# A fused attention and FFN kernel: the second batch's transposes begun one unit later, its loads put ahead of the output weights, and the first FFN unit spread one product per step

## The chip, the cores and the metric

The kernel runs on one core of a Trainium2 chip. The core has separate engines that run their own instruction streams in order: TensorE (PE in the profile; its weight loads PEld), VectorE (DVE), ScalarE (ACT), GpSimd (POOL), and SyncE (SP), which issues transfers. The metric is the device time of one launch in microseconds (us). The kernel before was timed three times: 394.67, 395.43 and 396.14, median 395.43 us.

## The reference

Block-sparse attention over 4 batches of 8 heads, 768 tokens and head size 64, then an RMS norm and a gated FFN over the 3072 tokens (model width 512, hidden width 1536). Cut to what is computed:

```python
scores = scale * np.matmul(q, k.transpose(0, 1, 3, 2))
# mask: neighbouring, first, last and sampled blocks of 32
scores = np.where(mask, scores, -1000000000.0)
scores = scores - np.max(scores, axis=-1, keepdims=True)
attn = np.exp(scores)
attn = attn / (np.sum(attn, axis=-1, keepdims=True) + 1e-09)
attn_out = np.matmul(attn, v)
...
x = attn_out.transpose(0, 2, 1, 3).reshape(B * S, H * D)
rms = np.sqrt(np.mean(x * x, axis=-1, keepdims=True) + 1e-06)
xn = x / rms * rms_g
g = xn @ w_gate
silu = g * (1.0 / (1.0 + np.exp(-g)))
val = xn @ w_val
out = silu * val @ w_out
```

Inputs and output are float32; the kernel's loads turn them into bf16 on the way in.

## The kernel before

**Units and steps.** A unit is one half (384 query tokens) of one batch: 8 units, u = 2b + half. In a unit there are four head pairs, so n = 4u + pair runs from 0 to 31. For each n there are six key tiles of 128, and each (n, tile) is a *step*: 192 steps, step = 6n + tile. `qk_exp` does a step's attention: two matmuls (the *score pair*, L243) into a tile `s_`, and one exponential on ScalarE (L247) into `pt`. Tiles `s_` come from the pool `ps_s`, which has two buffers (the *score buffers*), taken in turn; a third request waits until the first holder has been read.

**What a step carries beside its score pair.** A table `fixed`, filled by `at(step, cost, function, ...)`, lists the work that belongs to certain steps:

- `transposes(b, pr)` turns a head pair's q and k into the layout that the score pairs read: 24 small PE matmuls (L165) into a score buffer (tile `tqk`) and two copies on VectorE into `X` (L174). With `early` (batch 0) it uses the FFN's two buffers instead (tiles `tq`, `tk`, copies L171). `X` has six slots; pair pr of batch b is read from step 6(8b + pr) on.
- `av` and `zsum`, one step after a pair's last tile: the product with v (L264), copied to `osb` (L269) and squared by GpSimd (L270), and the sums of the exponentials (L280).
- `norm_a` to `norm_e`, the unit's normaliser: small matmuls (zt L300, ft L333, fb L351), a chain of small VectorE instructions and one on GpSimd (L315) that ends in FHL (L325), a copy `fs` on ScalarE (L337), and the scaled input `xn` of the FFN (L356). For unit 0 these use the FFN's buffers, for later units the score buffers. For unit u they stand at steps 24u + 28 to 24u + 36.
- `load_qk` and `load_v`, the transfers of a later batch, issued by GpSimd (L72, L73, L77).

**The FFN.** A *product* is a call of `ff_g` (four matmuls into `gp`, a tanh on ScalarE L375, `uu` on VectorE L377), `ff_v` (four into `vp`, `hp` on VectorE L391) or `ff_y` (three of the twelve matmuls of an output tile into `yp`, then `yo` and its store). `gp` and `vp` have one buffer each. Unit u's products go into a queue at step 37 + 24u (START is 37), 24 of `ff_g` and `ff_v`, and from u = 1 on the 12 `ff_y` of the unit before. In each step the scheduler takes products off the queue by a *credit*: every step adds a rate worked out from the estimated costs, and all work subtracts its cost (0.34 for a score pair, 0.65 for a product). `RESERVE` keeps five products in the queue while there are attention steps. In units after the first, a step is also filled until its estimated work reaches 0.9.

**The order of the engines.** All instructions are written out in this order, and each engine runs its own in that order. Thus a PE instruction that waits for a transfer holds up every score pair behind it.

**The loads.** All loads of inputs but two small ones are issued by GpSimd into one queue (`software_dynamic`): batch 0's q, k and v, then the gate and value weights wg and wv in two halves each (`load_w`, L134 and L135), the output weights wo (`load_wo`, L138), and from step 3 on batch 1's q and k. Its v is loaded at step 24. Batch 1's transposes stand at steps 27, 33, 39 and 45; its first score pair is step 48.

Of the kernel before, what the change touches and what calls it, by code (L numbers as in the profile page):

```python
# [17 lines left out]
def kernel(  # L18
# [114 lines left out]
    def load_w(i):  # L133
        nc.gpsimd.dma_start(out=wg[:, :, i * FH:(i + 1) * FH], in_=wgv[:, :, i * FH:(i + 1) * FH])  # L134
        nc.gpsimd.dma_start(out=wv[:, :, i * FH:(i + 1) * FH], in_=wvv[:, :, i * FH:(i + 1) * FH])  # L135

    def load_wo():
        nc.gpsimd.dma_start(out=wo, in_=moe_w_out.rearrange("(c p) f -> p c f", p=P))  # L138
# [89 lines left out]
    nc.gpsimd.memset(nhalf, -0.5)  # L228
    load_w(0)
    load_w(1)  # L230
    load_wo()

    ptiles, osb, zwt, xns, hps, o2s = {}, {}, {}, {}, {}, {}

    def qk_exp(n, jt):
        u, pr = divmod(n, NP)
        b, ic = divmod(u, 2)
        sl = (b * NP + pr) % NSLOT
        if jt == 0:
            ptiles[n] = ppool.tile([P, NC, 2, TG], BF16, name="pt", tag="pt")  # L240
        s_ = ps_s.tile([P, 2, 512], FP32, name="s_", tag="s")
        for e in range(2):
            nc.tensor.matmul(  # L243
                out=s_[:, e, 0:TG],
                lhsT=X[0:D + NB, sl, e, 1, jt * P:(jt + 1) * P],
                rhs=X[0:D + NB, sl, e, 0, ic * TG:(ic + 1) * TG], start=True, stop=True)
        nc.scalar.activation(  # L247
            out=ptiles[n][:, jt, :, :], in_=s_[:, :, 0:TG], func=AF.Exp, scale=SCALE)
# [167 lines left out]
    NSTEP = NU * NP * NC  # L416
# [4 lines left out]
    def at(step, cost, fn, *a):  # L421
        fixed.setdefault(step, []).append((cost, fn, a))

    for n in range(NU * NP):
        u, pr = divmod(n, NP)
# [12 lines left out]
    at(0, 0, mask_rows, 2, 4)  # L438
    at(4, 0, mask_rows, 4, 2 * NSLOT)
    for b in range(1, B):  # L440
        for pr, sl in enumerate((4, 5, 6, 7) if b == 1 else (2, 4, 6, 7)):
            at(6 * (8 * (b - 1) + sl) + 3, 0.95, transposes, b, pr)
        at(6 * 8 * (b - 1) + 3, 0, load_qk, b, 0, H)
        at(6 * (8 * (b - 1) + 4), 0, load_v, b)

    ffq = []
    for u in range(NU + 1):
# [20 lines left out]
    step, credit = 0, 0.0  # L468
    queue = []
    while True:  # L470
        if step < NSTEP:
            qk_exp(step // NC, step % NC)
            credit -= 0.34
        since = 0.0
        for cost, fn, a in fixed.pop(step, ()):
            fn(*a)
            since += cost
        credit -= since
        u, r = divmod(step - START, 24)
        if u >= 0:  # L480
            if r == 0 and u < len(ffq):
                queue += ffq[u]
                if u == 0:
                    credit = 0.0
            credit += rate.get(u, 99.0)
            keep = RESERVE if step < NSTEP else 0
            while len(queue) > keep and (credit > 0 or (since < 0.9 and step < NSTEP and u > 0)):
                cost, fn, a = queue.pop(0)
                fn(*a)
                credit -= cost  # L490
                since += cost
            if len(queue) <= keep:
                credit = min(credit, 0.0)
        step += 1
        if step >= NSTEP and not fixed and not queue and u >= NU:
            break
# [30 lines left out]
```

## Time and profile before

| | us |
|---|---|
| median of three runs | 395.43 |
| the profiled execution | 396.17 |
| its span, first to last instruction | 394.4 |
| PE busy | 355.1 |
| DVE busy | 211.4 |
| ACT busy | 201.7 |
| POOL busy | 61.2 |

The profile comes from one execution of its own, with the device time and the span given here. Busy times count instructions; a PE matmul's end is modelled, so short gaps between matmuls can be missing or show as busy. In the rows of the timeline, the first number is the start in us from the span's start, the second the length, and the bracket gives how long the engine was idle before and what released it; "x12" is a group of twelve. In the rows of waits stand the waiting and the awaited instruction, the total, the times and the longest. The page's slices are 9.86 us each, in tenths of busy time; PEclk is the granted clock of PE in tenths.

### The profile page before, as it was taken

The numbers are of one execution on the slowest core, as the hardware profiler recorded it, in microseconds if no ns is written. First come the engines' busy times: TensorE is split into PE (matmuls) and PEld (weight loads), VectorE is DVE, ScalarE is ACT, GpSimd is POOL, SyncE is SP. The second block draws the span as 40 slices with busy tenths as digits, with TensorE's granted clock in tenths as the row PEclk, the third lists the DMA queues.
The fourth block names the chain that finished last, engine by engine and source line by source line (L and its number), as shares of the span: only waits on it lengthen the run. The fifth ranks groups of instructions, "written<-read, shape, count | busy, mean of one in ns | idle before, by whom it ended". The sixth has DMA issues, their size and how long they took to land.

```text
span 394.4 us, 6579 instructions
## 1 busy us (share of the span) xinstructions
PE 355.1 (90%) x2700; PEld 189.8 (48%) x2730; DVE 211.4 (54%) x411; ACT 201.7 (51%) x302; POOL 61.2 (16%) x88
## 2 busy tenths in 40 slices
PE   2887068889799999999999999999999999999995
PEld 1443033445355555555555555555555555455552
DVE  5651035655354665556564666556544564587660
ACT  2677035556555555555656565555556656322211
POOL 8952001002101010021001110001000100000000
PEclk9999559999899999999999999999999999999999
DMA  5999950004605100009006000000000000000002
GB/s 72 175 210 208 205 90 2 1 2 68 94 2 71 37 27 2 28 28 161 27 28 107 1 28 13 15 29 27 2 27 29 2 27 28 27 28 27 28 27 106
DMA packets 20257, 20.86 MB, mean 53 GB/s; under 512 B 1284, under 2 KB 17156, under 8 KB 20228
## 3 DMA queue, kind: packets, MB, share of 16 engines
q0 software_dynamic: 16208, 14.16, 23.3%
q1 hardware_dynamic: 4020, 6.30, 4.2%
q8 instruction: 21, 0.34, 0.3%
q14 instruction: 8, 0.07, 0.1%
HBM read 28.31 MB, written 6.29 MB: 88 GB/s over the span
## 4 chain that ended last, share of the span: by engine, by line
PE 72%; DMA 8%; DVE 6%; POOL 5%; ACT 5%; issue 2%; POOLq 0%; DVEq 0%; ACTq 0%
PE gp L371 14%; PE vp L388 14%; PE yp L402 13%; DMA kb<-in_k_dram 7%; PE zw L280 4%; ACT pt L247 3%; DVE xn L356 2%; PE tqk L165 2%; PE oa L264 1%; PE zt L300 1%; PE fb L351 1%; DVE uu L377 1%; ACT th L375 1%; DMA out_dram<-yo 1%; PE vw L388 1%
## 5 line engine op out<-in xcount | busy, mean ns | idle before, releaser
L377 DVE SCALAR_TENSOR_TENSOR uu<-th,gp 128x384 bf16<-128x384 bf16 x90 | 49.8, 554 | 71.0 <-ACT th L375 70.2
L371 PE MATMUL gp<-xn,wg 128*128 128x384 bf16 x360 | 73.2, 326 | 1.4 <-DVE uu L377 1.2
L388 PE MATMUL vp<-xn,wv 128*128 128x384 bf16 x360 | 73.2, 325 | 0.9 <-DVE hp L391 0.9
L402 PE MATMUL yp<-wo,hp 128*128 128x512 bf16 x258 | 70.7, 379 | 1.8 <-issue 0.3
L375 ACT ACTIVATE th<-gp 128x384 bf16<-128x384 f32 x90 | 44.0, 489 | 50.5 <-PE gp L371 49.8
L243 PEld LDWEIGHTS <-X 88*128 88x128 bf16 x384 | 35.3, 100 | 51.1 <-issue 23.9
L391 DVE TENSOR_TENSOR hp<-uu,vp 128x384 bf16<-128x384 bf16 x90 | 49.9, 554 | 17.5 <-PE vp L388 8.7
L371 PEld LDWEIGHTS <-wg 128*128 128x128 bf16 x384 | 36.7, 98 | 32.1 <-issue 3.8
L388 PEld LDWEIGHTS <-wv 128*128 128x128 bf16 x384 | 37.0, 97 | 26.5 <-issue 1.9
L402 PEld LDWEIGHTS <-hp 128*128 128x128 bf16 x288 | 27.6, 97 | 24.9 <-issue 0.8
L174 DVE COPY X<-tqk 64x1536 bf16<-64x1536 bf16 x26 | 24.8, 954 | 24.7 <-PE tqk L165 24.4
L264 PEld LDWEIGHTS <-vb 128*64 128x64 bf16 x384 | 21.5, 114 | 18.1 <-issue 11.1
L280 PE MATMUL zw<-pt,Ez 128*32 128x384 bf16 x384 | 22.4, 341 | 0.0
L165 PE MATMUL tqk<-ident,qb 128*64 128x128 bf16 x156 | 7.5, 236 | 15.0 <-DMA qb<-in_q_dram 14.0
L356 DVE SCALAR_TENSOR_TENSOR xn<-osb,gcol,fb 128x384 bf16<-128x384 f32 x28 | 15.9, 610 | 5.9 <-PE fb L351 5.9
L315 POOL TENSOR_TENSOR rs<-ms,nhalf 128x3 f32<-128x3 f32 x8 | 6.9, 866 | 67.3 <-DVE ms L312 67.3
L411 DVE TENSOR_SCALAR yo<-yp 128x512 f32<-128x512 f32 x21 | 14.4, 686 | 5.4 <-PE yp L402 5.3
L165 PEld LDWEIGHTS <-qb 128*64 128x64 bf16 x192 | 6.8, 119 | 20.1 <-DMA qb<-in_q_dram 14.4
L280 PEld LDWEIGHTS <-Ez 128*32 128x32 bf16 x384 | 7.4, 97 | 12.6 <-issue 11.0
L264 PE MATMUL oa<-pt,vb 128*64 128x384 bf16 x96 | 11.3, 379 | 0.0
L165 PE MATMUL tqk<-ident,kb 128*64 128x128 bf16 x156 | 7.3, 234 | 4.0 <-DMA kb<-in_k_dram 4.0
L269 DVE COPY osb<-oa 128x384 f32<-128x384 f32 x8 | 4.5, 557 | 10.3 <-PE oa L264 10.3
(557 smaller groups left out, 461.7 us busy)
## 6 DMA issues: line engine op xcount, KB each, us to landing
out_dram<-yo SPq DMA_DIRECT2D x24, 256.0 KB, 2.0
vb<-in_v_dram POOLq DMA_DIRECT2D x4, 768.0 KB, 8.1
qb<-in_q_dram POOLq DMA_DIRECT2D x3, 768.0 KB, 7.4
kb<-in_k_dram POOLq DMA_DIRECT2D x3, 768.0 KB, 10.8
wg<-in_moe_w_gate_dram POOLq DMA_DIRECT2D x2, 768.0 KB, 12.8
wv<-in_moe_w_val_dram POOLq DMA_DIRECT2D x2, 768.0 KB, 15.3
wo<-in_moe_w_out_dram POOLq DMA_DIRECT2D x1, 1536.0 KB, 23.4
qb<-in_q_dram POOLq DMA_DIRECT2D x2, 192.0 KB, 3.5
```

The costliest lines, as they stand in the source:

```text
L165: nc.tensor.transpose(out=tt[i][64 * h:64 * h + 64, c * P:(c + 1) * P], in_=src[:, 2 * pr + h, c * D:(c + 1) * D], identity=ident)
L174: nc.vector.tensor_copy(out=X[0:D, sl, h], in_=t_[64 * h:64 * h + 64, :, 0:S])
L243: nc.tensor.matmul(out=s_[:, e, 0:TG], lhsT=X[0:D + NB, sl, e, 1, jt * P:(jt + 1) * P], rhs=X[0:D + NB, sl, e, 0, ic * TG:(ic + 1) * TG], ...
L264: nc.tensor.matmul(out=o_[64 * e:64 * e + 64, :], lhsT=vb[:, 2 * pr + e, jt * D:(jt + 1) * D], rhs=pt_[:, jt, e, :], start=(jt == 0), stop ...
L280: nc.tensor.matmul(out=zwt[u][32 * c:32 * c + 32, :], lhsT=Ez[:, pr, :], rhs=pt_[:, 2 * j2 + par, e, :], start=(pr == 0 and j2 == 0), stop ...
L356: nc.vector.scalar_tensor_tensor(out=xns[u][:, pr, :], in0=osb[u][:, pr, :], scalar=gcol[:, pr:pr + 1], in1=fb[i], op0=ALU.mult, op1=ALU.mult)
L371: nc.tensor.matmul(out=gp, lhsT=wg[:, c, f * P:(f + 1) * P], rhs=xns[u][:, c, :], start=(c == 0), stop=(c == NP - 1))
L375: nc.scalar.activation(out=th, in_=gp, func=AF.Tanh, scale=0.5)
L377: nc.vector.scalar_tensor_tensor(out=uu, in0=th, scalar=1.0, in1=gp, op0=ALU.add, op1=ALU.mult)
L388: nc.tensor.matmul(out=vp, lhsT=wv[:, c, f * P:(f + 1) * P], rhs=xns[u][:, c, :], start=(c == 0), stop=(c == NP - 1))
L391: nc.vector.tensor_tensor(out=hps[u][:, f, :], in0=uu, in1=vp, op=ALU.mult)
L402: nc.tensor.matmul(out=yp, lhsT=hps[u][:, f, t * P:(t + 1) * P], rhs=wo[:, f, :], start=(f == 0), stop=(f == NF - 1))
```

## The change

Three edits, all in the order of the work; no instruction is added or removed.

1. `load_wo` is no longer issued behind `load_w` but at step 7, and batch 1's v at step 6 instead of 24, so that q, k and v of batch 1 stand ahead of wo.
2. Batch 1's transposes go from steps 27, 33, 39 and 45 to 45, 51, 57 and 63. Step 63 also holds, as before, the first set of batch 2.
3. The rule that fills a step: a step takes a product, whatever the credit and the reserve, while its estimated work beside the score pair is under 0.5 (0.9 in a step with `norm_d` or `norm_e`), in unit 0 too.

```diff
     load_w(0)
     load_w(1)
-    load_wo()
...
-        for pr, sl in enumerate((4, 5, 6, 7) if b == 1 else (2, 4, 6, 7)):
+        for pr, sl in enumerate((7, 8, 9, 10) if b == 1 else (2, 4, 6, 7)):
             at(6 * (8 * (b - 1) + sl) + 3, 0.95, transposes, b, pr)
         at(6 * 8 * (b - 1) + 3, 0, load_qk, b, 0, H)
-        at(6 * (8 * (b - 1) + 4), 0, load_v, b)
+        at(6 * (8 * (b - 1) + (1 if b == 1 else 4)), 0, load_v, b)
+    at(7, 0, load_wo)
...
-        since = 0.0
+        since, gap = 0.0, 0.5
         for cost, fn, a in fixed.pop(step, ()):
             fn(*a)
             since += cost
+            if fn in (norm_d, norm_e):
+                gap = 0.9
...
-            while len(queue) > keep and (credit > 0 or (since < 0.9 and step < NSTEP and u > 0)):
+            while (len(queue) > keep and credit > 0) or (queue and since < gap and step < NSTEP):
```

On GpSimd, the issue of loads behind the gate and value weights, before:

```order
L134 DMA wg<-in_moe_w_gate_dram 128x4x768
L135 DMA wv<-in_moe_w_val_dram 128x4x768
L138 DMA wo<-in_moe_w_out_dram 128x12x512
L72 DMA qb<-in_q_dram 128x8x384
L73 DMA kb<-in_k_dram 128x8x384
L270 TENSOR_TENSOR o_283<-osb 128x384 x3
L77 DMA vb<-in_v_dram 128x8x384
```

and after (one line fewer ahead of it, so L270 is now L269):

```order
L134 DMA wg<-in_moe_w_gate_dram 128x4x768
L135 DMA wv<-in_moe_w_val_dram 128x4x768
L72 DMA qb<-in_q_dram 128x8x384
L73 DMA kb<-in_k_dram 128x8x384
L77 DMA vb<-in_v_dram 128x8x384
L269 TENSOR_TENSOR o_284<-osb 128x384
L138 DMA wo<-in_moe_w_out_dram 128x12x512
```

The output weights moved behind three loads of batch 1 and the first square.

On VectorE, from the last `osb` copies of unit 0 into its normaliser (zs, zc, rz), before; the `X<-tqk` row is the copies of batch 1's transposes of step 27:

```order
L269 COPY osb<-oa 128x384 x2
L174 COPY X<-tqk 64x1536 x2
L293 COPY zs<-zw 128x384
L304 COPY zc<-zt 128x48
L306 RECIPROCAL rz<-zc 128x24
```

and after:

```order
L268 COPY osb<-oa 128x384 x2
L292 COPY zs<-zw 128x384
L303 COPY zc<-zt 128x48
L305 RECIPROCAL rz<-zc 128x24
L307 TENSOR_TENSOR w_565<-zc,rz 128x24
```

The copies, and PE's transposes that they follow, left this stretch, as did those of step 33 a little further on.

They stand now further on, among the products. On VectorE, from unit 1's FHL (step 56) to step 64, before:

```order
L325 TENSOR_TENSOR FHL_200<-fx,FHL_200 128x3x8
L269 COPY osb<-o__1097 128x384
L356 SCALAR_TENSOR_TENSOR xn<-osb,gcol,fb 128x384 x4
L269 COPY osb<-o__1166 128x384
L391 TENSOR_TENSOR hp<-uu,vp 128x384
L377 SCALAR_TENSOR_TENSOR uu<-th,gp 128x384
L174 COPY X<-tqk 64x1536 x2
```

and after:

```order
L324 TENSOR_TENSOR FHL_200<-fx,FHL_200 128x3x8
L268 COPY osb<-o__1058 128x384
L390 TENSOR_TENSOR hp<-uu,vp 128x384
L174 COPY X<-tqk 64x1536 x2
L355 SCALAR_TENSOR_TENSOR xn<-osb,gcol,fb 128x384 x2
L376 SCALAR_TENSOR_TENSOR uu<-th,gp 128x384
L390 TENSOR_TENSOR hp<-uu,vp 128x384
L355 SCALAR_TENSOR_TENSOR xn<-osb,gcol,fb 128x384 x2
L268 COPY osb<-o__1175 128x384
L376 SCALAR_TENSOR_TENSOR uu<-th,gp 128x384
L390 TENSOR_TENSOR hp<-uu,vp 128x384
L174 COPY X<-tqk 64x1536 x4
```

The copies of step 57's transposes stand ahead of unit 1's first xn, products stand between its two halves, and step 63's two sets of transposes bring four copies in a row.

In steps, the products of unit 0 are spread so. Before: 24 products over steps 37 to 64, with steps 53 to 61 empty of products while five are held back, three in step 37, and two each in steps 41, 42, 47, 48, 51, 62 and 64. After: 24 products over steps 37 to 59, three in step 37, two each in steps 38, 40, 41, 42, 46 and 48, and one at most in each of steps 49 to 61; unit 1's first products come at step 62 instead of 65, and by the end of step 64 four products of the next unit are done.

## The prediction, made before the changed kernel was run

> **What bounds the kernel now.** I read the page's header, busy times and slices first, to see where the span is not TensorE (PE) work.
>
> ```profile
> span 394.4 us, 6579 instructions
> ...
> PE 355.1 (90%) x2700; PEld 189.8 (48%) x2730; DVE 211.4 (54%) x411; ACT 201.7 (51%) x302; POOL 61.2 (16%) x88
> ...
> PE   2887068889799999999999999999999999999995
> ...
> PEclk9999559999899999999999999999999999999999
> ```
>
> From the twelfth slice on PE is full; what can be won lies ahead of it. Slice 5 has no PE work at all, slices 5 and 6 run at half the granted clock, and slice 11 dips. The waits between 38 and 120 us name the hole:
>
> ```profile
> ACT pt L247 <- PE s__565 L243: 13.5, 1, 13.5
> ...
> PE tqk L165 <- DMA qb<-in_q_dram: 9.2, 1, 9.2
> ...
> PE tqk L165 <- DMA kb<-in_k_dram: 3.0, 1, 3.0
> ```
>
> PE waits 12.2 us for batch 1's q and k, and the exponentials wait for PE. The chain that ended last runs through the same transfer, and the timeline shows the place: step 27's transposes stand in PE's queue ahead of step 28's score pair (s__565).
>
> ```profile
> 22.56 29.26 DMA kb<-in_k_dram
> ```
>
> ```profile
> 38.28 0.49 PE L243 MATMUL s__534<-X 88*128 88x384 bf16 x2
> ...
> 39.19 0.81 ACT L247 ACTIVATE pt<-s__534 128x768 bf16<-128x768 f32 x1
> 48.00 0.85 PE L165 MATMUL tqk<-ident,qb 128*64 128x128 bf16 x12 [9.23 <-DMA qb<-in_q_dram]
> 51.86 0.85 PE L165 MATMUL tqk<-ident,kb 128*64 128x128 bf16 x12 [3.01 <-DMA kb<-in_k_dram]
> 52.65 0.82 PE L243 MATMUL s__565<-X 88*128 88x384 bf16 x2
> ```
>
> Cutting the span at the starts of score pairs gives the stages (columns: stretch, its length, then busy time of PE, PEld, DVE, ACT, POOL, then granted clock and DMA): the hole; steps 28 to 36; 37 to 51; 52 to 60; 61 to 64; the saturated rest.
>
> ```profile
> 39.30:52.65 13.35, 1.64 (x25) 1.23 (x25) 0.00 (x0) 0.69 (x1) 0.00 (x0) 0.55 1.30 204
> 52.65:66.44 13.79, 11.77 (x85) 5.84 (x84) 7.96 (x18) 7.05 (x10) 1.71 (x2) 0.69 0.11 17
> 66.44:93.73 27.29, 25.08 (x224) 13.50 (x222) 15.21 (x25) 15.76 (x25) 3.46 (x5) 1.00 0.00 1
> 93.73:105.27 11.54, 8.57 (x65) 4.48 (x64) 6.06 (x18) 8.26 (x13) 2.51 (x3) 1.00 0.94 138
> 105.27:115.19 9.92, 9.01 (x77) 4.75 (x76) 5.18 (x9) 4.01 (x6) 0.83 (x1) 0.83 0.00 0
> 115.19:343.00 227.81, 224.32 (x1728) 122.25 (x1753) 129.55 (x254) 131.30 (x197) 26.10 (x31) 1.00 0.15 33
> ```
>
> **Term A: the hole and steps 28 to 36.** The transposes of steps 27 and 33 leave this stage, so nothing in it needs a transfer. Step 28 would follow step 27 at 39.3. From there to step 37's pair (66.44) the kernel before takes 27.14 us, about half of it at a low clock. What the nine steps take at full clock is read from the stage just ahead, where ScalarE's exponentials set the pace:
>
> ```profile
> 32.33 0.50 PE L243 MATMUL s__476<-X 88*128 88x384 bf16 x2
> ...
> 33.72 0.48 PE L243 MATMUL s__484<-X 88*128 88x384 bf16 x2 [0.57 <-ACT pt L247]
> 34.42 0.48 PE L243 MATMUL s__488<-X 88*128 88x384 bf16 x2 [0.22 <-ACT pt L247]
> ...
> 37.95 0.50 PE L243 MATMUL s__530<-X 88*128 88x384 bf16 x2
> ```
>
> Six steps with one `av` and `zsum` take 5.62 us (32.33 to 37.95) and three plain ones 2.1 (0.70 each), 7.7 together. Unit 0's normaliser lies here too. At full clock (unit 1's) its chain on VectorE and GpSimd, from the first zt matmul to FHL, takes 3.8 us:
>
> ```profile
> 96.14 0.74 PE L300 MATMUL zt<-Sel,zs 128*128 128x16 f32 x6
> ...
> 99.73 0.18 DVE L325 TENSOR_TENSOR FHL_200<-fx,FHL_200 128x24 bf16<-128x24 f32 x1
> ```
>
> From zt's start PE has 0.74 of zt, two pairs (0.33 each, 91.77 to 92.10 below) and `av` and `zsum` (1.70, 90.07 to 91.77), 3.1 us, so `norm_d` at step 32 waits near 0.7; with half a us for the scale copy that ScalarE must make I take 1.2 in all. That is 8.9 us: step 37 at 48.2 instead of 66.44, a gain of **18.2**. Bounds: 7.7 us, if the normaliser is hidden (gain 19.4); 13.8, if the stage goes on as slowly as its own row (gain 13.35).
>
> Does another load become late? Wv's second half lands last of the weights that the first products need, and wo ran ahead of q and k:
>
> ```profile
> 18.82 1.87 POOL L135 DMA_DIRECT2D wv<-in_moe_w_val_dram  x1
> ```
>
> ```profile
> DMA to landing us min/median/max: 12.8/15.3/17.7
> ```
>
> ```profile
> wo<-in_moe_w_out_dram POOLq DMA_DIRECT2D x1, 1536.0 KB, 23.4
> ```
>
> The longest of wv's landings, 17.7, on 18.82 gives 36.5, well ahead of the first product near 49. qb and kb land 3.9 apart (48.00, 51.86), so wo, twice the size, accounts for about 7.7: kb lands near 44, vb near 48, wo near 56. They are wanted at steps 45 (near 65), 55 and 64. The reordering of the queue thus hides behind the later transposes: even kb at 51.86 would be in time. GpSimd's issue of vb moves ahead of its first square and wo's behind it; nobody waits for that square before `norm_a`. I cost the queue at nothing; if its order cost anything, wo has 30 us of slack.
>
> **Term B: steps 37 to 64.** Before, this is 48.75 us (27.29 + 11.54 + 9.92), with 24 products and three sets of transposes; afterwards 28 products and five sets. The four extra products come out of the saturated rest one for one, so they cancel. The rows for the rest:
>
> ```profile
> 86.37 0.81 PE L371 MATMUL gp<-xn,wg 128*128 128x384 bf16 x4
> 87.03 0.81 PE L388 MATMUL vp<-xn,wv 128*128 128x384 bf16 x4
> ...
> 88.34 0.81 PE L371 MATMUL gp<-xn,wg 128*128 128x384 bf16 x4 [0.18 <-DVE uu L377]
> ...
> 90.07 1.17 PE L264 MATMUL oa<-pt,vb 128*64 128x384 bf16 x12
> ...
> 91.77 0.50 PE L243 MATMUL s__1015<-X 88*128 88x384 bf16 x2
> 92.10 0.49 PE L243 MATMUL s__1019<-X 88*128 88x384 bf16 x2
> ...
> 100.44 0.33 PE L333 MATMUL ft<-ident,FHL_200 128*128 128x128 bf16 x3 [0.61 <-DVE osb L269]
> ...
> 105.91 2.13 PE L264 MATMUL o__1166<-pt,vb 128*64 128x384 bf16 x12
> ...
> 109.02 0.50 PE L243 MATMUL s__1193<-X 88*128 88x384 bf16 x2
> ...
> 111.08 0.53 PE L165 MATMUL tqk<-ident,qb 128*64 128x128 bf16 x12
> ...
> 111.87 0.82 PE L388 MATMUL vp<-xn,wv 128*128 128x384 bf16 x4
> 111.98 1.92 DVE L174 COPY X<-tqk 64x1536 bf16<-64x1536 bf16 x2
> ```
>
> Added:
> - Two sets of transposes that lay in the first hole and its wake: 0.79 each (111.08 to 111.87), 1.6.
> - Each set keeps one of the two score buffers until both its copies are done (1.92). PE has a pair and two products (about 1.6) to run meanwhile, so some 0.4 shows, twice: 0.8.
> - Step 58's `norm_e` wants the buffer held by step 57's transposes; a pair alone lies between. 1.92 less 0.33, less what the copies overlap: 1.2.
> - Step 63 has two sets in a row, which hold both buffers, so step 64's pair waits for the first's copies: 1.92 less the second set's 0.79, with the release 1.3.
>
> Sum +4.9. Removed:
> - Idle PE in steps 52 to 64, now filled by the products that the reserve held back: 11.54 − 8.57 and 9.92 − 9.01, 3.9.
> - The clock dip: `av` and `zsum` took 3.11 us there (105.91 to 109.02) against 1.70 at full clock (90.07 to 91.77), 1.4.
>
> Sum −5.3; **B is −0.4**. The third edit is not quite what its words say: steps 38, 40, 41, 42, 46 and 48 still get two products, and such a step lasts 1.97 (86.37 to 88.34) where its work is about 1.63; the kernel before has about as many, so I count nothing. Bounds: −3.7 if no buffer wait shows; +4.9 if idle time and dip only move elsewhere.
>
> **Term C: the rest.** The same work in another interleaving. The row has 227.81 − 224.32, 3.5 us, of idle PE; I take 0, between −3.5 and as much lost again.
>
> Sum: 394.4 − 18.2 − 0.4 = 375.8 of span. The profiled execution took 396.17, 1.77 more than its span, and the median of the runs, 395.43, lies 0.74 below it: 375.8 + 1.77 − 0.74 = **376.8**. All bounds at once give 368.8 and 390.5.
>
> **A rule against the trace.** With no long hole left, does the clock still dip? Ahead of 105.27 PE never waited longer than the 0.61 us of the row at 100.44, yet 105.27 to 115.19 was granted 0.83. The Trainium skill, "TensorE: Matmul & The Clock Gate", section "HAM oscillation — how this bites in real kernels", puts the condition as "no PE-idle gaps >~3.4µs." By that the sum stands and the first rival is impossible; the trace differs, so I keep the rival.
>
> **The rivals.**
> 1. *The clock dips once more*, in steps 33 to 40, where pairs and a few small matmuls make a thin stream as at 100 to 105. For: that dip. Against: the bare pairs from 33.72 on are as thin and kept their clock (PEclk 9). One or two dips of 1.4 to 1.7: 378.3 to 380.3.
> 2. *VectorE's copies become the wait.* Batch 1's transposes now come three steps before their use, and each copy pair queues behind uu and hp. For: 1.92 us on VectorE against about 3.4 between (steps 51 to 54: 1.1 with the transposes, then 1.3 and 1.0 with one product each). If each of four sets costs 1 to 1.3 beyond B: 380.8 to 382.
> 3. *More is won*: the buffer waits hide behind products and some of C's idle goes, 2.3 to 4.3 beyond B and C as taken: 372.5 to 374.5.
> 4. *The wait moves to wg and wv* at step 37, so that the change doesn't do what it says. The landing at 36.5 speaks against it; it decides from a landing past 50, and gives back one for one: at 58, 385.
> 5. *Slower*: the clock stays at half through steps 37 to 64, as in 39.30 to 52.65 (0.55). `av` and `zsum` gain 1.4 on 1.70, so every us of PE work at half costs about 0.8; the gain of 18.6 is gone after 23 us of such work, and the whole stage would add 34, 411 (about 42 us of work: 28 pairs, 28 products at 0.65, five `av` and `zsum`, five sets, the normaliser). Against: PEclk is back at 9 from the seventh slice (59 us) on, and steps 37 on are dense.
>
> **How the numbers follow.** Forecast, 374.5 to 378.3: 0.62. Rivals: 1, 0.16; 2, 0.09; 3, 0.09; 4, 0.01; 5, 0.03. The range 372.5 to 381.5 leaves out 5, 4 and part of 2 and of the outer bounds. About 0.5% (2 us) is what a measurement of this kernel tells from no change: faster 0.96, same 0.01, slower 0.03.
>
> **What would show it.** Right: no PE wait for qb or kb behind 20 us; step 37's pair near 48 instead of 66.44, its first product 2 us later; slice 5 of PE at 7 or more and PEclk at 9 throughout; step 64's pair near 97. Wrong: a wait of PE for wg or wv, PEclk of 5 past slice 5, PE waits for VectorE's X copies above 1 us at steps 48, 54 and 60, or more than 3.5 us of idle PE behind step 65.

## The result and the profile after

The changed kernel took a median of 380.31 us (378.11 to 381.61, four runs) against 395.46 before: a ratio of 0.961, 95% interval 0.956 to 0.967, so 15.2 us were won where 18.6 were forecast (376.8 us, range 372.5 to 381.5). Run again beside the experiments it took 379.24 (0.960, 0.958 to 0.963). Both lie inside the range but above the 374.5 to 378.3 that the prediction held likeliest, where its first rival put the time (378.3 to 380.3).

The page of the profiled execution, which took 381.61 us, the longest of the four. Header, PE's busy time, PE by slices, its granted clock:

```profile
span 379.9 us, 6604 instructions
...
PE 352.9 (93%) x2730; PEld 187.9 (49%) x2730; DVE 210.1 (55%) x411; ACT 200.5 (53%) x302; POOL 60.9 (16%) x88
...
PE   2998889988899999999999999999999999999995
...
PEclk9999999999999999999999999999999999999999
```

The empty slice and the long half-clock stretch are gone. PE's largest waits between 38 and 120 us are now these (waiter, awaited, total, times, longest):

```profile
PE gp L370 <- DVE uu L376: 1.1, 4, 0.5
PE ft L332 <- DVE osb L268: 1.1, 1, 1.1
PE s__1280 L242 <- DVE X L174: 1.1, 1, 1.1
PE fb L350 <- ACT pt L246: 0.9, 1, 0.9
```

No wait for q or k is left. The third is step 64's pair behind step 63's double transposes, the fourth `norm_e` at step 58. PE's timeline gives the borders of the stages: the pairs of steps 27, 28, 37, 64 and 65, and the first product:

```profile
40.55 0.49 PE L242 MATMUL s__534<-X 88*128 88x384 bf16 x2
41.61 0.48 PE L242 MATMUL s__538<-X 88*128 88x384 bf16 x2 [0.57 <-ACT pt L246]
...
50.27 0.48 PE L242 MATMUL s__651<-X 88*128 88x384 bf16 x2
...
52.39 0.82 PE L370 MATMUL gp<-xn,wg 128*128 128x384 bf16 x4
...
98.97 0.50 PE L242 MATMUL s__1280<-X 88*128 88x384 bf16 x2 [1.05 <-DVE X L174]
...
100.61 0.49 PE L242 MATMUL s__1297<-X 88*128 88x384 bf16 x2
```

Cut there, the profile of the same kernel's second execution (span 377.0) gives steps 28 to 36, 37 to 64, and the rest (columns as in the prediction):

```profile
38.73:47.40 8.67, 7.30 (x59) 3.62 (x59) 3.95 (x14) 7.07 (x11) 1.71 (x2) 1.00 1.30 205
47.40:97.73 50.33, 44.45 (x425) 25.00 (x424) 31.91 (x57) 28.72 (x43) 6.82 (x8) 1.00 0.37 58
97.73:377.00 279.27, 270.63 (x1999) 145.71 (x1996) 154.89 (x308) 141.64 (x219) 26.95 (x32) 1.00 0.14 35
```

The first execution had 8.66, 50.34 and 279.29 for the same three. The stages repeat to 0.02 us; the whole difference between the two executions, 2.9 us, lies ahead of step 28. About half of it (1.4 us, 8.45 instead of 7.01 from step 20 to step 28) is a half-clock stretch of the first one that the page's slices are too coarse to show:

```profile
35.00:40.00 5.00, 4.34 (x31) 1.67 (x29) 0.43 (x1) 3.16 (x5) 0.00 (x0) 0.66 1.32 205
```

### The profile page after: what moved, and what is told of

Its sections match the earlier page's. It is cut to its first block, busy times and chain, and to the rows that moved or that the text cites. A ratio compares the mean times of both kernels' runs of the same rounds, so it can differ in the third digit from the quotient of the medians.

```text
span 379.9 us, 6604 instructions
## 1 busy us (share of the span) xinstructions
PE 352.9 (93%) x2730; PEld 187.9 (49%) x2730; DVE 210.1 (55%) x411; ACT 200.5 (53%) x302; POOL 60.9 (16%) x88
## 4 chain that ended last, share of the span: by engine, by line
PE 76%; DVE 10%; ACT 6%; issue 3%; DMA 2%; POOL 1%; POOLq 0%; DVEq 0%
PE yp L401 14%; PE gp L370 14%; PE vp L387 13%; PE zw L279 5%; ACT pt L246 3%; PE oa L263 3%; ACT th L374 2%; DVE uu L376 2%; DVE xn L355 2%; DVE X L171 2%; PE tqk L165 1%; DVE X L174 1%; DMA kb<-in_k_dram 1%; DMA out_dram<-yo 1%; PE vw L387 1%
## 5 line engine op out<-in xcount | busy, mean ns | idle before, releaser
L401 PE MATMUL yp<-wo,hp 128*128 128x512 bf16 x288 | 75.9, 379 | 0.0
L269 POOL TENSOR_TENSOR o_1613<-osb 128x384 bf16<-128x384 f32 x4 | 3.3, 826 | 30.3 <-DVE osb L268 30.3
```

Of the source, the lines that this page charges most:

```text
L401: nc.tensor.matmul(out=yp, lhsT=hps[u][:, f, t * P:(t + 1) * P], rhs=wo[:, f, :], start=(f == 0), stop=(f == NF - 1))
```

## The experiments

Each edit below is against the changed kernel, or against the kernel before where it is said. Times are medians; a set's own runs of the kernel before stand beside it (395.51, 395.94 and 395.89 us in the three sets).

### The changed kernel again

No edit.

> The changed kernel once more, beside the three below. Its first times were 378.1 to 381.6 us with the clock at 1.000 in the shortest. Theory: the 2.3 us that the profiled run lost ahead of step 28 (pairs at 33.16 instead of 32.33 us at step 20, 40.22 instead of 37.95 at step 26) come from when the clock rises and dips, which differs from execution to execution; so its times spread over about 3 us, and 379.5 +- 1 is the median. Rival: the loss is the changed order of the loads; then every execution has step 26 near 40.2 us and none is near 378.

Measured: 379.24 us (378.73 to 380.81), with mean granted clocks of 1.000, 0.998, 1.000, 0.995 and 0.995; the two at 0.995 are the two near 380.8. In its profile step 20's pair stood at 31.72 us and step 26's at 37.34, against 33.16 and 40.22 in the first one, with the loads in the same order. The rival falls.

### The transposes alone

The kernel before, with one line changed:

```diff
-        for pr, sl in enumerate((4, 5, 6, 7) if b == 1 else (2, 4, 6, 7)):
+        for pr, sl in enumerate((7, 8, 9, 10) if b == 1 else (2, 4, 6, 7)):
```

> Only batch 1's transposes at steps 45, 51, 57, 63; loads and product rule as before. Theory: the later transposes alone take the wait away, since kb landing at 51.86 us is ahead of step 45 near 66; no PE wait for qb or kb, term A (18 us) is won whole, and what is missing to the changed kernel is term B's filling of steps 53 to 61, about 2 us less its stalls: 378 to 382 us. Rival: the loads must be moved as well; then PE waits for kb again and the time is above 385.

Measured: 384.76 us (0.973, 0.971 to 0.975). No PE wait for qb or kb behind 20 us is in its profile, so the mechanism holds; the size is off, 2.8 us beyond the upper end. Its windows over steps 28 to 36, then 52 to 60 and 61 to 64, show where:

```profile
39.47:49.37 9.90, 8.84 (x60) 4.07 (x60) 3.95 (x14) 6.96 (x11) 1.71 (x2) 0.83 1.30 205
...
77.58:90.84 13.26, 9.10 (x84) 4.55 (x84) 7.86 (x18) 7.57 (x10) 2.00 (x3) 0.95 0.82 120
90.84:102.22 11.38, 10.11 (x97) 5.37 (x97) 6.08 (x9) 3.62 (x5) 0.83 (x1) 0.75 0.00 0
```

With the old rule nothing fills steps 53 to 60: the transposes' waits stand there bare, and the clock falls to half behind them (0.75), as it did in the kernel before. The first stage has a dip of its own (0.83), which accounts for 1.2 of the 2.8 us. All four runs read 0.987.

### The loads alone

The kernel before, with edit 1 (`load_wo` at step 7, batch 1's v at step 6).

> Only the output weights moved behind batch 1's q, k and v; transposes at steps 27 to 45 and product rule as before. Theory: kb lands 43 us after the start instead of 51.86, so the hole shrinks from 13 to about 4.5 us: 395.5 less 8.7, 387, and down to 383 if the clock then doesn't fall to half. Rival (the queue's order doesn't set the landing): kb near 52 and the time within 1 us of 395.5.

Measured: 387.66 us (0.980, 0.978 to 0.983), the theory's 387. PE's timeline at step 27:

```profile
37.03 0.49 PE L242 MATMUL s__534<-X 88*128 88x384 bf16 x2
39.03 0.53 PE L165 MATMUL tqk<-ident,qb 128*64 128x128 bf16 x12 [1.51 <-DMA qb<-in_q_dram]
42.85 0.85 PE L165 MATMUL tqk<-ident,kb 128*64 128x128 bf16 x12 [3.30 <-DMA kb<-in_k_dram]
43.64 0.82 PE L242 MATMUL s__565<-X 88*128 88x384 bf16 x2
```

The queue does land in its order: kb comes 9 us earlier, and the hole shrinks to 1.51 and 3.30. The matmuls behind it still run at half clock (0.82 instead of 0.5).

### The product rule alone

The kernel before, with edit 3.

> Only the new product rule; transposes at steps 27 to 45 and wo ahead of batch 1's loads, as before. The hole at 39 us stays. Theory: the rule fills steps 53 to 59, worth the idle time and the clock dip there (3.9 and 1.4 us), and loses up to 2.7 in the later units, whose last steps it leaves with fewer products: 391 to 393.5 us. Rival: the rule is worth in itself what e1 lacks to the changed kernel, 5.5 us: 390 or less.

Measured: 392.33 us (0.991, 0.989 to 0.994): 3.6 us, within the theory's 391 to 393.5.

### Transposes and rule, without the loads

```diff
     load_w(1)
+    load_wo()
...
-        at(6 * (8 * (b - 1) + (1 if b == 1 else 4)), 0, load_v, b)
-    at(7, 0, load_wo)
+        at(6 * (8 * (b - 1) + 4), 0, load_v, b)
```

> The changed kernel with the loads in the order of before (wo ahead of batch 1's q and k, v at step 24). Theory: with the transposes late nobody waits for these loads (kb lands near 52 us, step 45 is near 65), so it is within 1 us of the changed kernel, 378 to 380.5. Rival: e1 lost 5.5 us against the changed kernel partly by its loads; then this is 382 or more.

Measured: 378.99 us (0.957, 0.955 to 0.960), no different from the changed kernel. Behind the late transposes the order of the loads is worth nothing. Alone, edits 2 and 3 are worth 10.8 and 3.6 us, together 17.0: the rule also covers the waits that the transposes bring along, and the dip behind them.

### The old rule in the later units

```diff
-            while (len(queue) > keep and credit > 0) or (queue and since < gap and step < NSTEP):
+            while ((len(queue) > keep and (credit > 0 or (since < 0.9 and step < NSTEP and u > 0)))
+                   or (queue and since < gap and step < NSTEP and u == 0)):
```

> The changed kernel, but its new product rule holds only in steps 37 to 60 (unit 0); later units are filled to 0.9 with the reserve of five, as before. Theory: the 2.7 us that the stretch behind step 65 lost come from the new rule, which leaves one product instead of two beside the normalisers of later units (waits of av for xn, of ft for osb, of vp for hp); so this is 1.5 to 2.7 us faster than the changed kernel. Rival: they come from the different order of gate, value and output products or from the clock, and this is within 0.7 us of the changed kernel.

Measured: 381.04 us (0.964, 0.961 to 0.966): 1.8 us worse, so the theory's time falls. The products done ahead leave unit 1 short of products, and with the reserve steps 82 to 84 then get none. PE's timeline from the first fb of unit 2's normaliser on:

```profile
130.18 0.49 PE L350 MATMUL fb<-fs,SelB 128*128 128x384 bf16 x2
131.29 0.48 PE L242 MATMUL s__1693<-X 88*128 88x384 bf16 x2 [0.63 <-ACT pt L246]
132.23 0.49 PE L242 MATMUL s__1698<-X 88*128 88x384 bf16 x2 [0.45 <-DVE xn L355]
132.67 0.48 PE L350 MATMUL fb<-fs,SelB 128*128 128x384 bf16 x2
133.67 0.78 PE L242 MATMUL s__1707<-X 88*128 88x384 bf16 x2 [0.52 <-ACT pt L246]
134.39 2.13 PE L263 MATMUL o__1711<-pt,vb 128*64 128x384 bf16 x12
```

The waits stand bare, and behind them the clock dips again (`av` 2.13 us instead of 1.17). All five of its runs read 0.995 or 0.996. Here the missing products were the cover of unit 2's normaliser. But only the time falls. From step 109 on, where the products stand in the order of before again, the stages take what they took before the change, and `av` waits for no xn (the table under Term C below). From there to the end it does two products more than the changed kernel in 0.6 us less. There the theory holds; the loss ahead of step 109 hides it.

### The normaliser's first matmul one step later

```diff
-            at(s1 + 8, 0.3, norm_d, u)
+            at(s1 + 9, 0.3, norm_d, u)
```

> The changed kernel with norm_d of every unit one step later (step 24u + 33). Theory: behind step 65 the changed kernel lost 2.7 us in small waits at the normalisers, the largest of them of ft for the osb copy and FHL (0.6 to 1.1 us a unit), because fewer products stand there; one step more lets that chain end first, 1.5 to 3 us faster, 376.5 to 378. Rival: the wait only moves on to fb and xn, one step closer to their use, and the time is within 0.7 us of the changed kernel.

Measured: 376.81 us (0.953, 0.950 to 0.957), 2.2 us below the kernel without the loads, which ran in the same set (0.955 to 0.960, so that the intervals overlap). The stage settles it: the rest behind step 65 takes 277.28 us instead of 279.27:

```profile
100.22:377.50 277.28, 270.10 (x1999) 145.77 (x1996) 154.82 (x308) 141.23 (x219) 26.95 (x32) 1.00 0.14 35
```

The theory holds; the wait of ft is gone from the profile and came back at fb only once, with 0.6 us.

### The transposes at steps 33, 45, 51 and 57

```diff
-        for pr, sl in enumerate((7, 8, 9, 10) if b == 1 else (2, 4, 6, 7)):
+        for pr, sl in enumerate((5, 7, 8, 9) if b == 1 else (2, 4, 6, 7)):
```

> The changed kernel with batch 1's transposes at steps 33, 45, 51 and 57 instead of 45, 51, 57 and 63. kb lands at 43 us, step 33 is near 45. Theory: the double set at step 63 and its wait for VectorE's copies (1.05 us) go, and one set (0.79 us) lies beside exponentials that set the pace: 1 to 2 us faster than the changed kernel, 377.5 to 378.5. Rival: the copies at step 33 hold a score buffer and stand ahead of unit 0's xn, which costs the thin stretch as much: within 0.5 us of the changed kernel, or slower by 1.

Measured: 377.87 us (0.955, 0.952 to 0.957), 1.1 us below the kernel without the loads, which ran in the same set; the intervals overlap here too. Counted from step 28's pair to the end it takes 337.24 us (376.3 − 39.06) against 338.27: 1.0 won. Both of its expectations were in part right: steps 37 to 64 give 1.35 back and the rest 1.46, while steps 28 to 36 take 10.45 instead of 8.67: VectorE's copies (1.92 us, from 46.20) stand ahead of unit 0's xn, which starts only at 48.16, and the second fb waits for it. One product more than in the changed kernel is done by the end of step 64 (29 instead of 28), so that 0.65 of the rest's 1.46 belongs to steps 37 to 64. All its runs read 0.998 or 0.999.

### Both together

> e6 and e7 together: batch 1's transposes at steps 33, 45, 51, 57 and norm_d one step later for every unit. Theory: the two gains lie in different stretches (step 63 and the normalisers behind step 65) and add: 379.3 less 1.6 less 2.5, about 375.2 us, 374 to 376.5. Rival: at step 33 norm_d of unit 0 now stands beside the transposes and its wait comes back there, so it is no faster than e7, 376.8.

Measured: 376.67 us (0.953, 0.950 to 0.955), just beyond the theory's 376.5; the times alone cannot tell it from `norm_d` alone (376.81), which is what the rival said. From step 28 to the end it takes 335.62 us (374.9 − 39.28), 2.65 less than the changed kernel and nearly the sum of both gains (1.0 and 2.0), so the theory holds there; two of its six runs read 0.995, near 378.6, and the four at 1.000 lie between 375.8 and 376.7.

### Extra matmuls in the thin steps

```diff
+    def keepwarm():
+        kw = ps_a.tile([P, 512], FP32, name="kw", tag="acc")[:, 0:TG]
+        for i in range(2):
+            nc.tensor.matmul(
+                out=kw, lhsT=X[0:D + NB, 0, i, 1, 0:P], rhs=X[0:D + NB, 0, i, 0, 0:TG],
+                start=True, stop=True)
...
+    for s in (21, 22, 23, 24, 28, 29, 33, 34, 35, 36):
+        at(s, 0, keepwarm)
```

> The changed kernel with two more matmuls of 384 columns in each of steps 21 to 24, 28, 29 and 33 to 36, into a tile that nobody reads: work is added, nothing is left out. Theory: about half of the changed kernel's executions lose 1.5 to 2 us to a half-clock stretch of PE between steps 24 and 37, where its stream is thin (times near 379 with the clock at 1.000 or 0.998, near 381 with 0.995). The extra matmuls fit in PE's slack (0.37 us a step) and keep the clock up: every execution at 0.998 or more, median 378 to 379, none above 380. Rival: the dip does not hang on how busy PE is there; then about half of the executions still show 0.995 and the median is 379.3 or more.

Measured: clocks of 0.998, 1.000, 1.000 and 1.000, so no run's clock shows the dip, as the theory had it; but 380.11 us (379.48 to 380.60), no faster, above its 378 to 379. The extra matmuls are not free: steps 28 to 36 took 9.35 us instead of 8.67. (Steps 20 to 27 took 7.02, as without them; that the profiled execution reached step 28 only at 39.95 comes from ahead of step 20.) Four runs without a dip, where about half would show one, support that it hangs on how dense the stream is; they don't prove it.

> e8 with the extra matmuls of e9. Theory: as e9 against the changed kernel, the slower executions of e8 go: 374 to 375.5 us with a spread under 1.5. Rival: with the transposes at step 33 the stretch is dense enough (e6 showed 0.998 or 0.999 in all executions), so that the extra matmuls only add work: equal to e8 or up to 1 us slower.

Measured, the extra matmuls on top of both: 375.73 us (0.952, 0.949 to 0.954; 375.33 to 377.74), clock 1.000 in all runs, but still two groups, near 375.6 and 377.7, so the theory's spread under 1.5 us is missed. The times are not distinguishable from those of the kernel without them (0.950 to 0.955). By stages the rival is right, the matmuls only add work: from step 28 to the end it takes 336.26 us (373.6 − 37.34) against 335.62.

## Why the prediction was right

**The mechanism.** Forecast right, and shown by the runs with parts of the change: PE's wait for q and k went and nothing took its place, the queue of loads is hidden, and faster by about 4% against 4.7% forecast. kb landed 43.2 us after the start (21.27 + 21.9), forecast near 44; the transposes need it at 67. The median came 3.5 us above the forecast. Of that, 1.2 lie in the span of the second execution, which had no dip (377.0 instead of 375.8: 2.7 more in Term C, 1.4 less in A, in B and ahead of step 28). Another 0.7 lie in what was added to the span (1.77 − 0.74 forecast, 1.73 measured), and 1.6 in the slower runs of the first set, three of which read 0.995 or 0.996 (380.31 instead of 378.73).

**Term A** was sized well: steps 28 to 36 took 8.66 and 8.67 us, forecast 8.9; step 32's ft waited 0.71, forecast near 0.7. Only its start was off in the first profile: step 28 came at 41.61 instead of 39.3. That is not the change: the second execution has 38.73.

**Term B** as well: steps 37 to 64 took 50.34 us with four products more, that is 2.6 us of work; forecast 48.75 − 0.4 + 2.6, 50.95. Singly: step 64's pair waited 1.05 for the copies (1.3 forecast). Step 58's fb waited 0.9 (1.2 forecast), but not for the reason given: in the second execution it started at 85.33, just behind the exponential of step 58's own pair (84.47 + 0.81), while step 57's copies ran until 85.80. It did not take the buffer of the transposes, though the score buffers were said to be taken in turn; that the size came near is luck.

**Term C was mis-sized.** It was taken at 0, "The same work in another interleaving", with the four extra products out of the rest "one for one". The rest should have shrunk from 279.2 us (394.4 − 115.19) to 276.6 and stayed at 279.3. The work did leave; the other interleaving cost 2.7 us, within the bound of 3.5. By steps, in us from score pair to score pair, with the products done there:

| steps | before | changed, second execution | changed, old rule in later units |
|---|---|---|---|
| 65 to 84 | 35.31 (31) | 35.24 (30) | 35.21 (27) |
| 85 to 108 | 42.99 (36) | 42.52 (35) | 44.39 (36) |
| 109 to 132 | 42.81 (36) | 42.53 (35) | 42.81 (36) |
| 133 to 156 | 42.97 (36) | 43.03 (36) | 42.98 (36) |
| 157 to 180 | 41.29 (36) | 41.68 (36) | 41.29 (36) |
| 181 to the end | 73.84 (89) | 74.27 (88) | 73.86 (89) |

At 0.65 us a product, the changed kernel lies 0.6, 0.2, 0.4, 0.1, 0.4 and 1.1 us above the kernel before. With the old rule in later units nothing is lost from step 109 on. PE's waits show what the loss consists of. Between 101 and 320 us in the changed kernel:

```profile
PE ft L332 <- DVE osb L268: 1.2, 2, 0.6
PE o__3817 L263 <- DVE xn L355: 0.5, 1, 0.5
PE o__2797 L263 <- DVE xn L355: 0.5, 1, 0.5
PE o__3334 L263 <- DVE xn L355: 0.5, 1, 0.5
PE o__2261 L263 <- DVE xn L355: 0.2, 1, 0.2
...
PE o__1729 L263 <- DVE xn L355: 0.2, 1, 0.2
```

and between 115 and 338 in the kernel before, where `av` waits for no xn:

```profile
PE ft L333 <- DVE osb L269: 0.6, 1, 0.6
```

and behind the last attention step, two waits of the changed kernel alone:

```profile
333.56 0.81 PE L387 MATMUL vp<-xn,wv 128*128 128x384 bf16 x4 [0.40 <-DVE hp L390]
...
343.32 0.81 PE L387 MATMUL vp<-xn,wv 128*128 128x384 bf16 x4 [0.41 <-DVE hp L390]
```

Together the new ones are 1.8 for xn (0.45 three times, 0.25 and 0.20 in the timeline), 0.6 for ft and 0.8 for hp: 3.2 us, a little more than the loss. They come with the new rule and not with the transposes: the product rule alone has the same waits for xn and hp (a rest of 278.2 us, where five products less than before would make 276.0), and the transposes alone have none of them and take 42.81, 42.88 and 41.28 us from step 109 to 180.

What the rule changed there is in part the number of products, in part their order. In steps 80 to 84, 104 to 108 and 128 to 132 the changed kernel has seven products beside the normaliser instead of eight, in the order in which the two kernels issue them. In steps 152 to 156 and 176 to 180 it has as many as before, step by step, but is one product further in the sequence. So the step ahead of the second `norm_e` ends in a gate product instead of an output product, and that product's uu on VectorE comes just ahead of xn. Step 156, before and after (second execution):

```profile
278.15 0.49 PE L351 MATMUL fb<-fs,SelB 128*128 128x384 bf16 x2
278.68 1.14 DVE L356 SCALAR_TENSOR_TENSOR xn<-osb,gcol,fb 128x384 bf16<-128x384 f32 x2 [0.54 <-PE fb L351]
```

```profile
259.93 0.49 PE L350 MATMUL fb<-fs,SelB 128*128 128x384 bf16 x2
260.33 0.55 DVE L376 SCALAR_TENSOR_TENSOR uu<-th,gp 128x384 bf16<-128x384 bf16 x1 [1.06 <-ACT th L374]
260.80 1.13 DVE L355 SCALAR_TENSOR_TENSOR xn<-osb,gcol,fb 128x384 bf16<-128x384 f32 x2
261.99 1.17 PE L263 MATMUL o__3334<-pt,vb 128*64 128x384 bf16 x12 [0.45 <-DVE xn L355]
```

From fb to xn it is 0.53 us before and 0.87 after, and `av`, which takes a score buffer, now waits 0.45 us for xn. No run changed the order of the products alone, so how the 2.7 us divide between number and order is not shown. Moving ft gives 2.0 us back, though it leaves the waits for xn as they are.

The 3.5 us of idle time that Term C started from was over-read as well. Of PE's `yp` matmuls the profile before has 30 fewer records than that of the changed kernel, which does the same work (before, then after):

```profile
L402 PE MATMUL yp<-wo,hp 128*128 128x512 bf16 x258 | 70.7, 379 | 1.8 <-issue 0.3
```

```profile
L401 PE MATMUL yp<-wo,hp 128*128 128x512 bf16 x288 | 75.9, 379 | 0.0
```

So most of the 3.5 us between 115.19 and 343 is missing records: PE's waits there add up to 1.2 us. Over the same stretch of the changed kernel (to 5.0 us behind the last score pair, second execution) the subtraction gives 3.5 too (225.20 − 221.69), but there the waits add up to 3.4:

```profile
97.73:322.93 225.20, 221.69 (x1728) 119.82 (x1726) 125.59 (x249) 129.54 (x195) 25.42 (x31) 1.00 0.15 33
```

The sign that the prediction gave for this, "more than 3.5 us of idle PE behind step 65", could therefore not tell the two kernels apart; the rows of waits do.

**The first rival happened besides.** The clock dipped in about half of the executions: of 15 runs of the changed kernel and of the one without its loads, seven read 0.995 or 0.996 and eight 0.998 or 1.000. Both profiles taken of such a run have the dip in the thin stretch ahead of the first products, from step 25 in one and from step 31 in the other, somewhat earlier than the rival's steps 33 to 40. The stage of steps 28 to 36 with a dip took 9.89 us, 1.2 more:

```profile
39.46:49.35 9.89, 8.82 (x60) 4.09 (x60) 3.95 (x14) 6.96 (x11) 1.71 (x2) 0.83 1.30 204
```

(the kernel without the loads). It was priced at 1.4 to 1.7, near the 1.2 and 1.4 measured, but given only 0.16; the trace's argument against it, that the bare pairs from 33.72 us on had kept their clock, was one execution's luck. In the 10 us ahead of the first profile's dip PE's longest wait was 0.57 us:

```profile
34.56 0.48 PE L242 MATMUL s__486<-X 88*128 88x384 bf16 x2 [0.57 <-ACT pt L246]
...
36.67 0.80 PE L242 MATMUL s__499<-X 88*128 88x384 bf16 x2 [0.22 <-ACT pt L246]
```

So the Trainium skill's "no PE-idle gaps >~3.4µs" ("TensorE: Matmul & The Clock Gate", "HAM oscillation — how this bites in real kernels") doesn't cover it: here the clock fell with no wait longer than that. The density of the stream alone does not decide it either: from 30 to 35 us PE was busy 3.89 of 5 us in this execution and 3.99 in the second one, which kept its clock. A denser stream (8.87 of 10 us from 30 to 40 us with the extra matmuls, 8.13 in the second execution) showed no dip in any of the nine runs with them. What decides it in a given execution stays open.

The other rivals: the copies of VectorE cost no more than B had for them (1.05 us at step 64 is the largest); more than forecast was not won; no weight was late (first product at 52.39, wv's last half landed by 35 us, 18.54 + 16.5); the clock never stayed at half.

## What to carry to other kernels

A transfer that an in-order engine waits for is cheapest hidden by moving its consumer later; once that is done, moving the transfer as well brings nothing, though alone it was worth 8 us here. When work is pulled forward out of a saturated stage, ask which waits it covered there, and what will now stand ahead of each dependent instruction: the stage shrank by 2.7 us less than the work, and moving one dependent step back won 2.0. Compare stages between executions from a common instruction on: away from the clock's dips they repeated to 0.02 us, while the start varied by 2 to 3. And before idle time is read as busy time subtracted from a window, count the records: rows of waits are the safer measure.

## What the runs showed that was not expected

The first 15 to 23 us run at half rate (the rows show 0.80 us for a score pair, not 0.5) although the granted clock of these windows reads 1.00, and the end of it moves from execution to execution. The window of 10 to 20 us and step 8's pair, in the first profile of the changed kernel, and that pair in the kernel with the extra matmuls and both moves:

```profile
10.00:20.00 10.00, 9.48 (x60) 4.11 (x62) 6.95 (x8) 6.05 (x8) 9.49 (x20) 1.00 1.25 181
```

```profile
20.72 0.82 PE L242 MATMUL s__314<-X 88*128 88x384 bf16 x2
```

```profile
18.79 0.50 PE L249 MATMUL s__314<-X 88*128 88x384 bf16 x2
```

From there step 20 comes at 33.16 and 30.32 us: 2.8 us between two executions in a stretch whose PE work is the same in both. That is probably the larger part of the spread that remains where the clock reads 1.000 (375.33 to 377.74 us in the last kernel). The Trainium skill says of this rise that it is "run-variable: the window is free-running" ("TensorE: Matmul & The Clock Gate", "Part 1: The HAM clock gate (the "warmup" mystery)"); the runs agree that it varies. What sets the moment in a given execution was not tried.
